# Linear attention with a gated MLP on one core: a padded room in SBUF, gates stored from ScalarE's queue, and a third of wo loaded a round ahead

## The chip, the cores and the metric

The kernel runs on one core of a Trainium2 chip. The metric is the device time of one execution in microseconds (us), from the first instruction to the last, with what the device adds around it. TensorE (PE in the profile; its weight loads PEld) multiplies, VectorE (DVE), ScalarE (ACT) and GpSimd (POOL) work elementwise, and DMAs are issued by SyncE (SP) or, here in one stage before the change, by ScalarE. Each engine runs its own instructions in order. Data lies in SBUF, 128 partitions of rows, and matmuls write to PSUM. A matmul has a stationary operand, the weights, and a streamed one, here nearly always 128 partitions by 512 columns of 4 bytes.

## The reference

x is 2048 x 1024; there are 32 heads of 32; the inner width of the MLP is 3584.

```python
x = A_x
xn = _layernorm(x, axis=-1)
s = _A_ref(xn, A_wqkv, A_w_phi, A_wo)
g = _silu(_B_ref(xn, B_w1, B_w3, B_w2))
return x + s * g
```

`_A_ref` projects to q, k and v, maps q and k by a matrix for each head and a softmax of the result and of its negative (64 features), sums kv = phi_k^T v and z = sum of phi_k over all positions, and returns (phi_q kv) / (phi_q z + 1e-6) times wo. There is no causal mask. `_B_ref` is silu(xn w1) * (xn w3) times w2. Everything is float32.

## The kernel before

**Products.** A float32 number is split into a high part and a rest (`split`), and a product is three matmuls (`PASSES`: high by high, high by low, low by high). On top of that all large products use a two by two scheme with seven block products in place of eight. `ORDER` names them: left factors A11, A12, S2, S1, S3, S4, A22, right factors B11, B21, T2, T1, T3, B22, T4, and three PSUM banks a, b, c that sum them.

**Stages.** In order of time: gate and up (`gate_up`, matmuls in line 598), in two halves of tokens, each with 28 blocks of 128 columns of w1 and w3; the streamed operand is the normalized x, seven tiles `op0...` for the first half and `op1...` for the second, and the weights are `bo`. Then the heads in three rounds of eight pairs of token tiles: `heads` twice (line 794, streamed `op2...`, `op3...`, weights `xo`) for k and v, with the small matmuls of `kv` (line 779) between, and `query_heads` (line 861, `op4...`). Then the product with w2 (`product`, line 1195): seven rounds kb of eight pairs i of token tiles, one step for each; the streamed operand is `bo`, tiles of w2, the weights `af`, `as`. A step has seven block products of six matmuls (`TURN`); the products of A11, A12 and S2 belong to the new pair, the other four to the pair before, so that one more step with `new` None follows the last. Last comes attention (`attend`, line 1320) and the product with wo (`out_half`, line 1335), over 16 token tiles t, with 48 matmuls of 512 columns for each.

**Where tiles lie.** SBUF is filled by two stacks, one from each end. In the built program a row of each tile begins at these bytes of a partition; those of one pool follow each other in steps that are multiples of 512:

| pool | side | first byte | past a multiple of 512 | holds |
|---|---|---|---|---|
| misc | left | 1536 | 0 | `ident`, `consts` |
| small | left | 2560 | 0 | `early_z` first, then small tiles |
| work | left | 4992 | 384 | `w` and `h1` tiles, among them `as` for S2 |
| q | left | 19328 | 384 | quads: `bo` of gate and up, `xo`, `af`, `as`, `oT`, `g` |
| big, later acc | left | 64384 | 384 | `op` tiles in homes 0 to 6, later the 16 slabs |
| rb | left | 129920 | 384 | ring slots 8 to 19 |
| spare, later ra | right | 179712 | 0 | `op` tiles in homes 7 and 8, later ring slots 0 to 7 |
| rw | right | 212480 | 0 | raw weights, `ev`, `eq`; later `late` (ring slots 20, 21) and `room` |

`HOMES` says which operand lies where: all of op0 on the left; of op1 A11 and A12 on the right; of op2 T2 and T1; of op3 T3 and B22; of op4 none.

**The ring.** In the w2 stage `ring` hands out 22 slots of 4 KB a row in turn. A round of w2 takes 14. In the last round (kb = 6) the other eight go, in step i = 0, to `e0` (2), `kvs`, `own`, `ez` (2) and `xrs` (2). The 16 tiles of wo (`load_wo`) follow as the tiles of w2 are used up: six in step i = 7, eight in the step without a new pair, and two behind the loop.

**Gates.** The sums of pair i stand in two of the 16 slabs, by `SLABS[i]`. In the last round `gate(i - 2, j)` puts Silu over such a slab on ScalarE and stores it to `g_d` by SyncE, twice a step; those of pair 7 come behind the first attention. `load_g(t)` fetches gate and x of tile t again. Slabs that are free are used again: `load_e` fetches the query features of tile t into two of them, and `turn_e` transposes these into two others, from which `attend` streams.

```python
return slabs[:, (12, 14, 8, 10)[t % 4] + c] if t else e0[c]
```

**Order.** From line 1236 on the order on every engine is the program's own. In tile t of the attention stage stand, one behind the other: `out_half(t, 0)`, `load_e(t + 4)`, `scale` and `turn_e` of t + 1 on VectorE, for t + 3 >= 4 `z_products` on GpSimd, the rest of t - 1 (`gated`, `store_out`), `load_g(t + 1)`, `gated(t, 0)`, and then `attend(t + 1, ...)` around `out_half(t, 1)`; the low parts of `oT` (line 1326) come behind that on VectorE. SyncE issues the loads and stores in the same order, and one that waits holds up all behind it.

`early_z` is the room for the sums over features of the first four tiles (`EARLY`), which are made during the w2 stage. `edge_l` and `edge_r` are unused rooms at the two ends of SBUF; `PAD` is 32 and not used.

Of the kernel before, what the change touches and what calls it, by code (L numbers as in the profile page):

```python
# [8 lines left out]
F = mybir.dt.float32  # L9
# [8 lines left out]
P = 128  # L18
# [7 lines left out]
PAD = 32  # L26
# [3 lines left out]
def tile_kernel(ctx: ExitStack, tc: tile.TileContext, x, wkT, wqT, wv, wphi, wo, w1, w3, w2, out):  # L30
    nc = tc.nc
    open_pools = {}

    def pool(name, bufs, **kw):

        open_pools[name] = tc.tile_pool(name=name, bufs=bufs, reuse_waits="tile", **kw)
        return open_pools[name].__enter__()

    def close(*names):
        for name in names:  # L40
            open_pools.pop(name).__exit__(None, None, None)
# [23 lines left out]
    ANAMES, BNAMES = [n for _, n, _ in ORDER], [n for _, _, n in ORDER]  # L65

    pairs = [(8 * (i // 4) + i % 4, 8 * (i // 4) + i % 4 + 4) for i in range(NT // 2)]
# [3 lines left out]
    g_d = [dram.tile([P, D], F, name=f"g_d{i}") for i in range(NT)]  # L71
# [65 lines left out]
    small = pool("small", 2)  # L137
# [32 lines left out]
    def quad(name, dt=R):  # L170
        return qp.tile([P, 2, 4, P], dt, name=name, tag="q")
# [4 lines left out]
    def flat(t):  # L176
        return t.rearrange("p k t -> p (k t)")
# [1 line left out]
    ident = misc.tile([P, P], F, name="ident")  # L179
    consts = misc.tile([P, P], F, name="consts")  # L180
    eps_t = consts[:, 0:1]
    early_z = small.tile([P, 256], F, name="early_z", bufs=1)
    bd = bdp.tile([P, G, P], F, name="bd")

    def load_x(t, halves):
# [10 lines left out]
    def rstd(mv, sd=None):  # L196

        sd = small.tile([P, 4, 2], F, name="sd") if sd is None else sd
        var = mv[:, :, 1]
        nc.scalar.activation(sd[:, 0], var, AF.Sqrt, bias=eps_t)  # L200
        yield sd
        nc.vector.reciprocal(sd[:, 1], sd[:, 0])

        nc.vector.tensor_mul(sd[:, 2], sd[:, 1], sd[:, 1])
        nc.vector.scalar_tensor_tensor(sd[:, 3], var, EPS, sd[:, 2], op0=OP.add, op1=OP.mult)
        nc.vector.tensor_scalar(sd[:, 3], sd[:, 3], -0.5, 1.5, op0=OP.mult, op1=OP.add)
        nc.vector.tensor_mul(sd[:, 1], sd[:, 1], sd[:, 3])
        yield sd
# [186 lines left out]
    for tb in range(2):  # L395
        for f in range(NF):
            own = [at_event[tb, f, j] for j in range(7)]
# [279 lines left out]
    _, sd = rstd(mvs[0], sds[0])  # L677
# [245 lines left out]
    def ring(name):  # L923
        nonlocal ring_at
        k = ring_at % 22
        ring_at += 1
        if k < 20:
            return (bpa if k < 8 else bpb).tile([P, 2, 512], R, name=name, tag=f"ra{k}" if k < 8 else f"rb{k}")
        return late_rw[0][:, k % 2]
# [104 lines left out]
    bpb = pool("rb", 1)  # L1034
    slabs = accp.tile([P, 16, D], F, name="acc")

    SLABS = ((0, 1), (14, 15), (8, 9), (10, 11), (2, 3), (4, 5), (6, 7), (12, 13))

    def acc_of(i):
        return [slabs[:, m, c * 512:(c + 1) * 512] for m in SLABS[i] for c in range(2)]  # L1040

    for n in range(4, 7):
        load_b(0, n)

    wos, us, ezs = {}, {}, []
    EARLY = 4

    def load_wo(k):
        t = ring("wos")
        nc.sync.dma_start(t.bitcast(F), wo_d[k // 8][k % 8])  # L1050
        wos[k // 8, k % 8] = t

    def gate(i, j):
        m = SLABS[i][j]
        nc.scalar.activation(slabs[:, m], slabs[:, m], AF.Silu)
        nc.sync.dma_start(g_d[pairs[i][j]], slabs[:, m])

    def slot_f(name):
        return flat(ring(name).bitcast(F))

    def strips():
        for a in range(2):
            for s in range(2):
                yield a, s, slice(64 * a + 32 * s, 64 * a + 32 * s + 32)
# [18 lines left out]
    def load_kvs():  # L1083
        kvs = slot_f("kvs")
        for a, s, sl in strips():
            nc.sync.dma_start(kvs[sl].rearrange("p (j n) -> p j n", j=4), kv_d[:, :, s].rearrange("j f c g d -> f j (c g d)"))
        return kvs.rearrange("p (j c g d) -> p j c g d", j=4, c=2, g=4)
# [16 lines left out]
    def col(m):  # L1104
        return own[:, 64 * m:64 * m + 64]
# [44 lines left out]
    def factors(t):  # L1150
        if t < NT:
            nc.gpsimd.tensor_mul(col(0), col(3 + t % 2), w_all[:, 64 * t:64 * t + 64])

    def e_slab(t, c):
        return slabs[:, (12, 14, 8, 10)[t % 4] + c] if t else e0[c]

    def et_slab(t, c):
        return slabs[:, 2 * (t % 4) + c]

    def load_e(t):  # L1160
        for a, s, sl in strips():
            if t:
                m = (12, 14, 8, 10)[t % 4]
                nc.sync.dma_start(slabs[sl, m:m + 2].rearrange("i c (g n) -> i c g n", g=2), e_part(t, a, s))
            else:
                for c in range(2):
                    nc.sync.dma_start(halves(e0[c][sl]), e_part(0, a, s)[:, c])

    def scale(t, c):
        e = by_head(e_slab(t, c))  # L1170
        by = of_half(early(t) if t < EARLY else col(0), c)
        nc.vector.tensor_mul(e, e, by.unsqueeze(3).to_broadcast([P, 2, 16, DH]))
# [36 lines left out]
            nc.vector.tensor_add(c, pb, c)  # L1209


    steps = [(kb, i) for kb in range(NKB) for i in range(len(pairs))] + [None]
    TURN = (ORDER[3], ORDER[0], ORDER[4], ORDER[1], ORDER[5], ORDER[2], ORDER[6])
    FIRST = ("A11", "A12", "S2")
# [4 lines left out]

    for n in range(2 * EARLY):  # L1220
        at_ = 7 * 18 + 21 * n
# [15 lines left out]
    for r, new in enumerate(steps):  # L1237
        kb, i = new or (NKB, 8)
        end = kb >= NKB - 1
        if not end and i in (2, 3, 4, 5):  # L1240
            load_b(kb + 1, i - 2)
        if r + 2 < len(steps) - 1:
            ahead[r + 2] = load_h(*steps[r + 2])
        if r == 2:
            late_rw.append(rwp.tile([P, 2, 2, 512], R, name="late", tag="rw"))
            room_z = rwp.tile([P, 2, D], F, name="room", tag="rw")
            zb, er = room_z[:, 0], room_z[:, 1]
            w_all = er
        if r == 17:
            load_z()  # L1250
        if end:
            if i == 0:
                e0 = [slot_f("e0") for _ in range(2)]
                load_e(0)
                kvs, own = load_kvs(), slot_f("own")
                ezs += [slot_f("ez") for _ in range(2)]
                xrs = [slot_f("xr") for _ in range(2)]
            elif 3 < i < 7:
                load_e(i - 3)
        parts, bank = first, {}  # L1260
        if r and new:
            gen2 = second_parts(*parts)
        if r + 1 < len(steps) - 1:
            gen1 = first_parts(ahead.pop(r + 1))
        if kb and new:
            seed(i, bank, r)
        for m, (b, an, bn) in enumerate(TURN):
            if an in FIRST:
                if new:
                    product(kb, i, bank, r, parts[2], b, an, bn)  # L1270
            elif old:
                product(*old, banks, r, second, b, an, bn)
                if new is None:
                    for k in range(2 * BNAMES.index(bn), 2 * BNAMES.index(bn) + 2):
                        load_wo(k)
            if m < 3 and r and new:
                then = next(gen2)
            if m in (3, 4) and r + 1 < len(steps) - 1:
                first = next(gen1)
            if end and m in (1, 4) and 1 < i:  # L1280
                gate(i - 2, m // 4)
            if i + 1 == len(pairs) and an in FIRST:
                n = BNAMES.index(bn)
                for k in range(2):
                    if end:
                        load_wo(2 * n + k)
                    elif k:
                        load_b(kb + 1, 4 + n)
            for do in pieces.pop(7 * r + m, ()):
                do()  # L1290
        if new:
            second = then if r else ready[1]
        old, banks = new, bank
    for k in range(14, 16):
        load_wo(k)
    assert not pieces
    close("ps")


    ps = pool("ps4", 3, space=PSUM)  # L1300
    oTs, gs = {}, {}

    def load_g(t):
        if t < NT:
            gs[t] = flat(quad("g", F).rearrange("p u k t -> p u (k t)"))
            nc.sync.dma_start(gs[t], g_d[t])
            nc.sync.dma_start(xrs[t % 2], x[t * P:(t + 1) * P, :])


# [46 lines left out]
    for t in range(NT):  # L1356
        p, last = out_half(t, 0), t + 1 == NT
        if t + 4 < NT:
            load_e(t + 4)
        if not last:  # L1360
            for c in range(2):
                scale(t + 1, c)
        if t + 2 >= EARLY:
            weigh(t + 2)
        if not last:
            for c in range(2):
                turn_e(t + 1, c)
        if t + 3 >= EARLY:
            z_products(t + 3)
# [5 lines left out]
        store_out(t, 0)  # L1375
        if t + 2 >= EARLY:
            add_pairs(t + 2)
# [51 lines left out]
```

## Time and profile before

| what | us |
|---|---|
| median of 3 runs | 2409.21 (2408.97 to 2412.23) |
| the profiled execution | 2408.6 |
| its span, first to last instruction | 2406.8 |
| TensorE busy | 2371.8 |
| VectorE busy | 1763.1 |
| ScalarE busy | 909.5 |
| GpSimd busy | 257.2 |

The granted clock of TensorE is 0.999 of full speed over the span. 582 MB pass the DMA engines, 242 GB/s in the mean.

How to read it: a line of a view names an engine, a line of the kernel, and out<-in by the program's tile names without their numbers (op1A is op1A11, op1A12 and op1A22; bo is any tile of that name). Busy time is the union of the instructions' times. A single matmul is shown with some 390 ns, since its own time covers filling and draining the array, and the next one starts long before it ends; the pace is seen from when the next one starts. The chain of waits follows the work that ended last back from the end of the kernel; each piece has its start, its length and how many instructions are merged in it. "issue" is time in which an engine waited for nothing that the profile shows.

### The profile page before, as it was taken

What the parts mean: (1) busy time and instruction counts of PE and PEld (TensorE: products, weight loads), DVE (VectorE), ACT (ScalarE), POOL (GpSimd) and SP (SyncE); (2) the same over time, 40 slices, a digit from 0 to 9 for tenths busy, and PEclk for the clock granted to TensorE, in tenths of its full rate; (3) what the DMA queues carried; (4) which work ended last, traced back from release to release, by engine and by line L of the source; (5) the groups of instructions that cost most, each with busy time, mean ns of one, the idle gap of its engine ahead of it and who ended that gap; (6) DMA issues with size and microseconds to landing.
All of it is one profiled execution on the core that took longest, in us unless ns stands there. A gap on an engine that the chain in (4) does not pass through costs nothing.

```text
span 2406.8 us, 37213 instructions
## 1 busy us (share of the span) xinstructions
PE 2371.8 (99%) x14348; PEld 1934.4 (80%) x14348; DVE 1763.1 (73%) x2729; ACT 909.5 (38%) x1597; POOL 257.2 (11%) x243
## 2 busy tenths in 40 slices
PE   7999999999999999999999999999999999999999
PEld 6888888888788888888788788887888888886887
DVE  8877787765688888874566666786678888785775
ACT  6445454443344445542221212334433333352000
POOL 1000000000000000000000000331012222112662
PEclk9999999999999999999999999999999999999999
DMA  5446799976988888865977878986544554469773
GB/s 213 148 160 203 245 344 338 329 250 193 278 294 289 293 275 295 269 228 190 377 278 288 289 244 320 366 289 239 171 139 133 186 182 141 167 186 309 224 195 119
DMA packets 292625, 582.19 MB, mean 242 GB/s; under 512 B 25041, under 2 KB 140897, under 8 KB 289761
## 3 DMA queue, kind: packets, MB, share of 16 engines
q1 hardware_dynamic: 287840, 563.04, 69.4%
q10 hardware_dynamic: 4608, 16.78, 1.8%
q8 instruction: 113, 1.85, 0.3%
q14 instruction: 64, 0.52, 0.1%
HBM read 374.73 MB, written 205.00 MB: 241 GB/s over the span
## 4 chain that ended last, share of the span: by engine, by line
PE 91%; DMA 3%; DVE 3%; SPq 1%; ACT 1%; issue 1%; POOL 0%; DVEq 0%; ACTq 0%; POOLq 0%
PE bankb L598 24%; PE bankb L1195 13%; PE bankc L598 12%; PE bankb L794 7%; PE pm L1335 6%; PE bankc L1195 6%; PE banka L598 6%; PE bankc L794 3%; PE banka L1195 3%; PE bankb L861 3%; PE banka L794 2%; PE bankc L861 1%; PE pkv L779 1%; PE po L1320 1%; DMA g_d<-acc 1%; PE pw L247 1%
## 5 line engine op out<-in xcount | busy, mean ns | idle before, releaser
L93 DVE TENSOR_TENSOR bo<-rw,bo 128x512 fp32r<-128x512 f32 x336 | 230.8, 689 | 161.5 <-ACT bo L92 160.9
L1195 PE MATMUL bankb<-bo,as 128*128 128x512 f32 x960 | 238.3, 392 | 1.2 <-ACT acc L1201 1.2
L1195 PEld LDWEIGHTS bankb<-bo,as 128*128 128x128 f32 x960 | 180.1, 188 | 42.2 <-ACT acc L1201 1.6
L92 ACT CAST bo<-rw 128x512 fp32r<-128x512 f32 x336 | 206.4, 617 | 14.0 <-DVE w2o L93 4.4
L1335 PE MATMUL pm<-wos,oT 128*128 128x512 f32 x672 | 168.6, 399 | 4.5 <-DMA wos<-wo_d 2.7
L598 PE MATMUL bankb<-op0S,bo 128*128 128x512 f32 x672 | 164.7, 394 | 1.9 <-ACT op0S L92 1.2
L598 PE MATMUL bankb<-op1S,bo 128*128 128x512 f32 x672 | 161.8, 390 | 0.7 <-ACT u L633 0.7
L598 PE MATMUL bankc<-op0S,bo 128*128 128x512 f32 x672 | 162.4, 391 | 0.0
L598 PE MATMUL bankc<-op1S,bo 128*128 128x512 f32 x672 | 161.6, 389 | 0.5 <-DVE bo L93 0.5
L598 PE MATMUL bankb<-op1A,bo 128*128 128x512 f32 x672 | 159.9, 392 | 2.2 <-DVE bo L93 2.2
L598 PE MATMUL bankb<-op0A,bo 128*128 128x512 f32 x672 | 159.8, 392 | 0.8 <-DVE bo L93 0.5
L1195 PE MATMUL bankc<-bo,as 128*128 128x512 f32 x624 | 160.4, 392 | 0.0
L771 POOL MEMSET ev<- 128x32 f32 x32 | 4.1, 129 | 1438.4 <-DVE bo L93 1100.1
L1335 PEld LDWEIGHTS pm<-wos,oT 128*128 128x128 f32 x672 | 123.1, 188 | 36.9 <-DMA wos<-wo_d 5.7
L598 PEld LDWEIGHTS bankb<-op1A,bo 128*128 128x128 f32 x672 | 125.8, 188 | 31.2 <-DVE bo L93 2.6
L598 PEld LDWEIGHTS bankb<-op0S,bo 128*128 128x128 f32 x672 | 126.3, 190 | 29.1 <-ACT op0S L92 1.6
L598 PEld LDWEIGHTS bankb<-op1S,bo 128*128 128x128 f32 x672 | 126.1, 188 | 28.1 <-ACT u L633 1.1
L598 PEld LDWEIGHTS bankc<-op1S,bo 128*128 128x128 f32 x672 | 126.1, 188 | 27.1 <-DVE bo L93 0.9
L598 PEld LDWEIGHTS bankb<-op0A,bo 128*128 128x128 f32 x672 | 125.2, 188 | 27.0 <-DVE bo L93 0.8
L598 PEld LDWEIGHTS bankc<-op0S,bo 128*128 128x128 f32 x672 | 125.4, 188 | 25.8
L1195 PEld LDWEIGHTS bankc<-bo,as 128*128 128x128 f32 x624 | 117.1, 188 | 26.3
L1209 DVE TENSOR_TENSOR acc<-bankb,acc 128x512 f32<-128x512 f32 x152 | 102.4, 684 | 36.2 <-PE bankb L1195 34.6
(260 smaller groups left out, 4348.9 us busy)
## 6 DMA issues: line engine op xcount, KB each, us to landing
rw<-in_w SPq DMA_DIRECT2D x112, 512.0 KB, 4.5
hr<-h_d SPq DMA_DIRECT2D x56, 512.0 KB, 4.8
h_d<-h SPq DMA_DIRECT2D x111, 256.0 KB, 5.1
xoS<-xo_d0S SPq DMA_DIRECT2D x44, 512.0 KB, 6.2
xoS<-xo_d1S SPq DMA_DIRECT2D x44, 512.0 KB, 6.2
xoA<-xo_d0A SPq DMA_DIRECT2D x33, 512.0 KB, 5.1
xoA<-xo_d1A SPq DMA_DIRECT2D x33, 512.0 KB, 4.9
e_d<-eq ACTq DMA_DIRECT2D x32, 512.0 KB, 5.9
```

The source lines that it names most:

```text
L92: nc.scalar.copy(hi, src)
L93: (by or nc.vector).tensor_sub(lo, src, hi.bitcast(F))
L247: nc.tensor.matmul(pw[:, g, :], wr[:, g], bd[:, 4 * c + g, :], start=True, stop=True)
L598: nc.tensor.matmul(bank[b], bos[tb, f][bn][:, w, k], ao[an][:, u, k], start=first and n == 0, stop=LAST[b] == an and n == 11, skip_group_c ...
L771: nc.gpsimd.memset(v[:, :, DH:], 1.0)
L779: nc.tensor.matmul(pkv[sl, m], e[:, m // 4, (m % 4) * P + 32 * h:(m % 4) * P + 32 * h + 32], v[:, 4 * (m % 4) + h], start=first and m == 0 ...
L794: nc.tensor.matmul(bank[b], xo[an][:, u, k], wb[bn][:, w, k], start=an in ("A11", "A12", "S1") and n == 0, stop=LAST[b] == an and n == 11, ...
L861: nc.tensor.matmul(bank[b], xo[an][:, u, k], wb[bn][:, w, k], start=an in ("A11", "A12", "S1") and n == 0, stop=LAST[b] == an and n == 11, ...
L1195: nc.tensor.matmul(bank[b], t[:, u, pos + k], bos[kb, bn, k][:, w], start=first and n == 0, stop=LAST[b] == an and n == 5, skip_group_chec ...
L1209: nc.vector.tensor_add(c, pb, c)
L1320: nc.tensor.matmul(po[32 * j:32 * j + 32, a, 64 * k:64 * k + 64], kvs[sl, j, c, k], et[sl, :, 4 * k + j], start=True, stop=True, skip_grou ...
L1335: nc.tensor.matmul(p, oTs[t, h][:, a, k], wos[c, 4 * h + k][:, b], start=n == 0, stop=n == 3 * ND - 1)
```

## The change

`early_z` gets 32 more columns, 128 bytes a row, which are not used. Its pool then takes a multiple of 512 bytes (2560 for 2432), and all that follows it on the left stack moves up by 128 bytes: work, q, big, acc and rb.

The slabs of pair i are now 2i and 2i + 1. The gates of pairs 0 to 5 are stored by ScalarE's own queue, right behind the Silu; those of pairs 6 and 7 (tiles 10, 14, 11 and 15) stay in their slabs, and `load_g` fetches only x for them. The features of tile t (from 1 on) go to slabs 2 to 9 in turn, their transposes to slabs 0 and 1 or 10 and 11. In the last round `load_e(1)` to `load_e(3)` come one step later.

In step i = 0 of the last round the eight other slots go to `e0`, `kvs` and the first five tiles of wo. Six more tiles follow in step i = 7, five in the step without a new pair, and there the slots of the remaining used tiles go to `own` and `ez`; `xrs` come behind the loop.

```diff
-    early_z = small.tile([P, 256], F, name="early_z", bufs=1)
+    early_z = small.tile([P, 256 + PAD], F, name="early_z", bufs=1)[:, :256]
...
-    SLABS = ((0, 1), (14, 15), (8, 9), (10, 11), (2, 3), (4, 5), (6, 7), (12, 13))
-
     def acc_of(i):
-        return [slabs[:, m, c * 512:(c + 1) * 512] for m in SLABS[i] for c in range(2)]
+        return [slabs[:, 2 * i + j, c * 512:(c + 1) * 512] for j in range(2) for c in range(2)]
...
-    EARLY = 4
+    EARLY, KEPT, gs = 4, 6, {}
...
     def gate(i, j):
-        m = SLABS[i][j]
+        m, t = 2 * i + j, pairs[i][j]
         nc.scalar.activation(slabs[:, m], slabs[:, m], AF.Silu)
-        nc.sync.dma_start(g_d[pairs[i][j]], slabs[:, m])
+        if i < KEPT:
+            nc.scalar.dma_start(g_d[t], slabs[:, m])
+        else:
+            gs[t] = slabs[:, m]
...
+    def e_at(t):
+        return 2 + 2 * ((t - 1) % 4)
+
     def e_slab(t, c):
-        return slabs[:, (12, 14, 8, 10)[t % 4] + c] if t else e0[c]
+        return slabs[:, e_at(t) + c] if t else e0[c]

     def et_slab(t, c):
-        return slabs[:, 2 * (t % 4) + c]
+        return slabs[:, (0, 10)[t % 2] + c]
...
+    def late_slots(bn):
+        nonlocal own
+        n = BNAMES.index(bn)
+        if n < 5:
+            for k in range(5 + 2 * n, 7 + 2 * n):
+                load_wo(k)
+        elif n == 5:
+            load_wo(15)
+            own = slot_f("own")
+        else:
+            ezs.extend(slot_f("ez") for _ in range(2))
...
                 load_e(0)
-                kvs, own = load_kvs(), slot_f("own")
-                ezs += [slot_f("ez") for _ in range(2)]
-                xrs = [slot_f("xr") for _ in range(2)]
-            elif 3 < i < 7:
-                load_e(i - 3)
+                kvs = load_kvs()
+                for k in range(5):
+                    load_wo(k)
+            elif 4 < i < 8:
+                load_e(i - 4)
...
                 if new is None:
-                    for k in range(2 * BNAMES.index(bn), 2 * BNAMES.index(bn) + 2):
-                        load_wo(k)
+                    late_slots(bn)
...
                     if end:
-                        load_wo(2 * n + k)
+                        load_wo(5 + 2 * n + k)
...
-    for k in range(14, 16):
-        load_wo(k)
     assert not pieces
+    xrs = [slot_f("xr") for _ in range(2)]
...
     def load_g(t):
         if t < NT:
-            gs[t] = flat(quad("g", F).rearrange("p u k t -> p u (k t)"))
-            nc.sync.dma_start(gs[t], g_d[t])
+            if t not in gs:
+                gs[t] = flat(quad("g", F).rearrange("p u k t -> p u (k t)"))
+                nc.sync.dma_start(gs[t], g_d[t])
             nc.sync.dma_start(xrs[t % 2], x[t * P:(t + 1) * P, :])
```

More of the change, by code (lines that the diff above doesn't have):

```diff
@@ L1162, in load_e @@
             if t:
-                m = (12, 14, 8, 10)[t % 4]
+                m = e_at(t)
                 nc.sync.dma_start(slabs[sl, m:m + 2].rearrange("i c (g n) -> i c g n", g=2), e_part(t, a, s))
@@ L1209, in product @@
             nc.vector.tensor_add(c, pb, c)
+    def late_slots(bn):
[9 more added lines that the diff above has]
+            ezs.extend(slot_f("ez") for _ in range(2))
+    own = None
     steps = [(kb, i) for kb in range(NKB) for i in range(len(pairs))] + [None]
@@ L1293, in tile_kernel @@
         old, banks = new, bank
-    for k in range(14, 16):
-        load_wo(k)
     assert not pieces
+    xrs = [slot_f("xr") for _ in range(2)]
     close("ps")
     ps = pool("ps4", 3, space=PSUM)
-    oTs, gs = {}, {}
+    oTs = {}
     def load_g(t):
         if t < NT:
-            gs[t] = flat(quad("g", F).rearrange("p u k t -> p u (k t)"))
-            nc.sync.dma_start(gs[t], g_d[t])
+            if t not in gs:
+                gs[t] = flat(quad("g", F).rearrange("p u k t -> p u (k t)"))
+                nc.sync.dma_start(gs[t], g_d[t])
             nc.sync.dma_start(xrs[t % 2], x[t * P:(t + 1) * P, :])
```

## The prediction

> **What bounds the kernel now.** I read the page's first line of busy times, then the chain of waits that ended last, stage by stage.
>
> ```profile
> PE 2371.8 (99%) x14348; PEld 1934.4 (80%) x14348; DVE 1763.1 (73%) x2729; ACT 909.5 (38%) x1597; POOL 257.2 (11%) x243
> PE 91%; DMA 3%; DVE 3%; SPq 1%; ACT 1%; issue 1%; POOL 0%; DVEq 0%; ACTq 0%; POOLq 0%
> ```
>
> TensorE is busy 99% of the span and is 91% of the chain. So only two things can move the time by much: the pace of one matmul after another, and the few places where TensorE stands still. I looked for both.
>
> The pace first. In the chain a run of matmuls lasts until the next run starts, so its length divided by its count is the pace. Two windows of the gate and up stage (L598), one in each token half:
>
> ```profile
> 560.28 5.44 PE bankb L598 x24
> 565.72 2.72 PE banka L598 x12
> ...
> 781.25 2.80 PE banka L598 x12
> 784.05 2.73 PE bankb L598 x12
> ...
> 794.94 5.51 PE bankb L598 x24
> ```
>
> The same product A12 (bank a, 12 matmuls of 128x512) takes 2.72 us in the first half and 2.80 in the second: 226.7 against 233.3 ns each. Nothing waits in either. What differs is the place of the streamed operand: in the first half it lies in "big" (left stack of SBUF, rows that start 384 bytes past a multiple of 512), in the second half A11 and A12 lie in "spare" (right stack, rows that start at a multiple of 512). The weights lie in "q", left, at 384, in both. The heads stage (L794) shows the same in one token pair:
>
> ```profile
> 1255.01 2.72 PE banka L794 x12
> 1257.73 2.79 PE bankb L794 x12
> 1260.52 2.81 PE bankc L794 x12
> 1263.33 0.70 PE pkv L779 x59
> 1264.02 2.93 PE bankb L794 x12
> 1266.95 2.72 PE bankc L794 x12
> ```
>
> B21 (big, left) 2.72; T2 and T1 (spare, right) 2.79 and 2.81; T3 and B22 (big) again 2.93 and 2.72. The 2.93 follows the many small kv matmuls of L779: a restart costs 0.21 us even when the operand is on the left. The group rows of S1 by T1 in the two rounds of this stage agree, since T1 changes its place between them:
>
> ```profile
> L794 PE MATMUL bankc<-op2T,xoS 128*128 128x512 f32 x96 | 23.7, 395 | 0.0
> ...
> L794 PE MATMUL bankc<-op3T,xoS 128*128 128x512 f32 x96 | 23.1, 389 | 0.0
> ```
>
> It is slow in round 0 (op2, right) and fast in round 1 (op3, left). So it is the place and not the product. Every left operand shares its offset with the weights and runs at 226.7 ns; every right operand stands 128 bytes off and runs near 233.
>
> The standstills next. The longest are where the last product ends and attention starts (windows: span, TensorE busy, ..., granted clock, DMA share, GB/s), with the waits in 2150 to 2250:
>
> ```profile
> 2183.00:2193.00 10.00, 9.51 (x220) 6.93 (x219) 6.62 (x7) 3.66 (x5) 0.00 (x0) 1.00 1.03 418
> 2193.00:2203.00 10.00, 7.75 (x87) 4.47 (x87) 0.00 (x0) 0.58 (x1) 0.00 (x0) 1.00 1.03 417
> ...
> PE pm L1335 <- DMA wos<-wo_d: 2.7, 8, 0.8
> PE pm L1335 <- DVE oT L1326: 1.2, 1, 1.2
> ```
>
> The granted clock is 1.00, so the throttle has no part. The DMA engines are full for 20 us, wo tiles arrive late eight times, and VectorE reaches L1326 late, because the tile g ahead of it came late. The chain shows why:
>
> ```profile
> 2183.19 0.80 PE po L1320 x53
> ...
> 2196.73 10.01 DMA g_d<-acc
> ...
> 2208.71 5.43 DMA acc<-e_d
> ...
> 2224.97 0.85 PE po L1320 x49
> 2225.82 2.99 PE pm L1335 x12
> ...
> 2229.60 8.51 PE pm L1335 x36
> 2238.28 0.79 PE po L1320 x53
> ...
> 2251.52 0.79 PE po L1320 x53
> ```
>
> The last store of a gate takes 10 us in the full DMA queues; load_e(4), which reuses that pair's slabs, waits for them on SyncE, and behind it stand the next g and x.
>
> **The change, part by part.** The profiled execution took 2408.6 us (span 2406.8, 1.8 around it); the median of the runs is 0.6 above. The sum is made on 2408.6.
>
> *The pad.* 128 bytes more in the small pool move everything behind it on the left stack from 384 to 0 past a multiple of 512: work, q, big, acc, rb. The right stack stays at 0. So every streamed operand, left or right, then has the offset of its weights, and I take 226.7 ns for all of them.
> - L598, second half: per block of 128 columns the run with A11 falls from 5.51 to 5.44, A12 from 2.80 to 2.72, the run behind it from 2.73 to 2.72: 0.16 x 28 blocks = 4.5 us.
> - L794: T2 and T1 lose 0.07 + 0.09 = 0.16 in each of 8 pairs, T3 and B22 as much in the second round: 2.6 us.
> - L1195, where tiles of both stacks take turns in the ring. First and last rows of the stage and the starts of bank a in two pairs of neighbouring steps:
>
> ```profile
> L1195 PE MATMUL bankb<-bo,af x288: 387/392/502, 1639.1 to 2170.3; 128*128 128x512 f32 x144
> ...
> 1958.87 1.37 PE banka L1195 x6
> ...
> 1968.53 1.37 PE banka L1195 x6
> ...
> 2142.85 1.40 PE banka L1195 x6
> ...
> 2152.59 1.40 PE banka L1195 x6
> ```
>
> A step of 42 matmuls takes 9.66 or 9.74 us, against 42 x 0.2267 = 9.52; over 56 steps that is 7.8 to 12.3. The whole stage, 1639.1 to 2183.19, is 544.1 us against 2352 x 0.2267 = 533.1; of the 11.0 some waits and the early sums' matmuls stay. I take 9.
> - L1335: a run of 36 takes 8.51 = 3 x 2.72 + 0.21 (restart, as behind kv) + 0.14, a run of 12 takes 2.99 = 2.93 + 0.06; 0.20 x 16 tiles = 3.2. I take 3.
>
> Together 19 us. No trace here shows weights and operand both at 0, so the bounds are wide: with no gain 0, and with the full loss instead (below) minus 47.
>
> A rule of the Trainium skill speaks against this part. Its page "TensorE: Matmul & The Clock Gate", section "Step-by-step: what each phase is for", says that TensorE reads SBUF through two independent ports and that loading the next weights takes no read bandwidth from the matmul that runs. By it the place of an operand could not matter, and the 19 would be 0. The rows of 2.72 and 2.80 do not agree with that.
>
> *Gates by ScalarE's queue.* Twelve stores leave SyncE's queue. ScalarE already issues stores of this size in the query stage:
>
> ```profile
> L846 ACTq DMA_DIRECT2D e_d<-eq x32: 326/326/345, 1494.7 to 1646.3; - x32
> ...
> 2156.35 0.58 ACT L1184 COPY banka<-acc 128x512 f32<-128x512 f32 x1
> ...
> 2162.16 1.56 PE L1195 MATMUL banka<-late,af 128*128 128x512 f32 x6
> ```
>
> Each costs 0.33 us of ScalarE, and a short wait until its own Silu has written: 12 x 0.33 = 4 us of an engine that is 38% busy. Queued behind it are the seed of bank a and casts for the next step; the seed ends at 2156.93 and TensorE wants it at 2162.16. That slack of 5.2 us hides it: 0. Without cover it would be at most the 4 us. SyncE no longer stands in front of a Silu, so its e and h loads go out earlier, if anything.
>
> *Four gates kept, slabs renumbered, five wo tiles a round ahead.*
>
> ```profile
> 2111.00 0.99 SPq L942 DMA_DIRECT2D hr<-h_d  x2
> ...
> 2174.03 1.06 ACT L1055 ACTIVATE acc<-acc 128x1024 f32<-128x1024 f32 x1
> ...
> 2188.37 2.36 DVE L1175 STREAM_TRANSPOSE acc<-acc 128x1024 f32<-128x1024 f32 x2
> ...
> L1050 SPq DMA_DIRECT2D wos<-wo_d x14: 319/320/739, 2172.7 to 2191.8; - x14
> ...
> DMA to landing us min/median/max: 3.0/5.6/10.6
> ```
>
> Four stores and four loads of 512 KB go. load_e(4) now reuses pair 4's slabs, stored two steps earlier. The transposes of e(1) go into pair 5's slabs, whose second Silu ends at 2175.1; they ran at 2188.4 before, so there are 13 us for a store of g_d, which took up to 10.6 (last row). The five wo tiles go out ahead of two h loads that were issued at 2111.0. At up to 0.74 us for an issue h is 3.7 us later; it took no more than the 10.6 of the stores to land, and its first user stands behind bank a of step 50, two steps before the 2142.85 above, so at 2123.4: at 2125.3 in the worst case, 1.9 us late for ScalarE and VectorE, which work for the step after; 0 for TensorE. In the last step eleven tiles remain, and the last of them is issued where tile 11 was before.
>
> What it is worth: from the first to the fourth attend the old chain takes 2224.97 - 2183.19 = 41.8 us. Without waits that is 2 x 0.79 + 24 matmuls (two thirds of 8.51) = 7.3, and two tiles of 13.24 (2251.52 - 2238.28): 33.8. So 8.0 us are lost there, of which the idle rows name 2.7 + 1.2. I take 7 (bounds 2.7 and 8.0): e(4), g(0) and the wo tiles all come earlier than their users, but the DMA queue is still well filled until about 2195. Next late would be e(4) for GpSimd.
>
> Sum: 2408.6 - 19 - 7 = 2382.6, say 2383.
>
> **The rivals.**
> 1. *The offset itself is what is slow, not the difference.* If an operand row that starts at a multiple of 512 bytes runs at 233 whatever its weights' offset, the pad makes all operands slow. It decides from the first matmul of L598. For it: in this trace the two readings can't be parted, as all weights lie at 384. Against it: the run behind a slow one (2.73) and the run behind kv (2.93) are slow on the left too and settle, so two streams get in each other's way, rather than one start being bad. Price: 9840 matmuls of 512 columns x 0.08/12 = 66, less the 19 that are slow already: +47. 2408.6 + 47 - 7 = 2449.
> 2. *The pad does nothing for pace*, as where two ports never disturb each other and something else about the right stack is slow: 2408.6 - 7 = 2402. This is the result by the skill's rule above. Against it are left and right rows of the same product.
> 3. *The tail's wait moves rather than goes*: the DMA engines stay at 1.03 until 2203 with other tiles in them, or VectorE waits for pair 5's store. Then only the pace counts: 2408.6 - 19 = 2390.
>
> **How the numbers follow.** Forecast 0.70 (own range 2377 to 2390), rival 1 0.10, rival 2 0.11, rival 3 0.09. 2408.6 less 22 (every matmul of L1195 and L1335 improved to the full) and less 8 gives 2379, and some restarts may shrink as well: low 2375. The high end takes in rival 2: 2404. Rival 1 stays outside. Faster by over 0.2% (what a measurement of this kernel can tell) are the forecast, rival 3 and nearly all of rival 2: 0.87; within 0.2%, rival 2 with a smaller tail gain: 0.03; slower 0.10.
>
> **What would show it.** In the chain, bank a of L598 in the second half at 2.72 instead of 2.80 and T1 of the heads at 2.72 (2.80 everywhere is rival 1; unchanged, rival 2). A step of L1195 near 9.52. The wait of L1335 for wo gone, and 34 to 35 us from the first attend to the fourth (41 is rival 3). It would be wrong above all if operand and weights at the same offset 0 do not run as they do at 384.

## The result, and the profile after

The changed kernel takes 2379.76 us (median of 4 runs, 2379.66 to 2381.62) against 2409.27 for the kernel before (4 runs, 2408.97 to 2412.23). The ratio is 0.9877, with a 95% interval of 0.9860 to 0.9894. The forecast was 2383 in a range of 2375 to 2404. The profiled execution took 2381.62 us, with a span of 2379.8 and a granted clock of 0.999.

Two lines of the page of the changed kernel, the busy times and the shares of the chain of waits:

```profile
PE 2351.0 (99%) x14348; PEld 1934.9 (81%) x14348; DVE 1760.9 (74%) x2729; ACT 910.1 (38%) x1597; POOL 257.6 (11%) x243
...
PE 93%; DVE 3%; DMA 2%; ACT 1%; SPq 1%; issue 0%; POOL 0%; DVEq 0%; ACTq 0%; POOLq 0%
```

TensorE has the same 14348 matmuls and is busy 20.8 us less (2351.0 for 2371.8). So most of the gain is pace. The span fell by 27.0, so some 6 us more are time in which TensorE no longer stands still.

The chain of waits of the changed kernel, in the gate and up stage (L598), the heads (L794) and the stage of w2, where `product` is now line 1199:

```profile
655.92 5.44 PE bankb L598 x24
...
794.96 2.72 PE banka L598 x12
...
1113.82 5.44 PE bankb L598 x24
...
1242.87 2.93 PE bankb L794 x12
1245.80 2.72 PE banka L794 x12
1248.52 2.72 PE bankb L794 x12
...
1925.02 1.36 PE banka L1199 x6
...
1934.54 1.36 PE banka L1199 x6
```

Bank a of L598 in the second half takes 2.72 us for 2.80 and the run ahead of it 5.44 for 5.51. In the heads all runs but the one behind the kv matmuls take 2.72. A step of w2, from bank a to bank a, takes 9.52 us for 9.66 or 9.74: exactly 42 times 226.7 ns. In the groups of the changed kernel the slow row of the heads has become like the fast one (23.1 us for 23.7):

```profile
L794 PE MATMUL bankc<-op2T,xoS 128*128 128x512 f32 x96 | 23.1, 389 | 0.0
...
L1199 PE MATMUL bankb<-bo,af x288: 388/389/500, 1629.1 to 2152.3; 128*128 128x512 f32 x144
```

Now the tail: the chain of the changed kernel (`attend` is L1336, `out_half` L1351, the low part of oT L1342, the first `gated` L1359), and its windows (span, TensorE busy, weight loads, VectorE, ScalarE, GpSimd, clock, DMA share, GB/s).

```profile
2164.89 1.64 PE po L1336 x106
2166.53 5.83 PE pm L1351 x24
2172.36 0.79 PE po L1336 x53
...
2179.95 0.16 DVE g L1359
...
2180.55 0.69 DVE oT L1342
...
2181.29 5.30 PE pm L1351 x22
...
2199.74 0.79 PE po L1336 x53
2200.53 2.95 PE pm L1351 x12
...
2204.27 8.43 PE pm L1351 x36
```
```profile
2165.00:2175.00 10.00, 10.00 (x224) 7.86 (x210) 6.55 (x7) 3.67 (x5) 0.00 (x0) 1.00 0.99 384
2175.00:2185.00 10.00, 9.07 (x99) 6.90 (x99) 5.05 (x6) 0.59 (x1) 2.12 (x1) 1.00 1.05 279
```

From 2164.89 to 2199.74 are 34.85 us, the stretch that the prediction called "first to fourth attend" (41.8 before, 33.8 without waits). What is left of the loss stands at 2179.95: VectorE waits there for the gate of tile 0, works on it, and only then makes the low part of oT that TensorE waits for. (The load of that gate goes out at 2167.18. Its landing is not recorded; that it ends the wait is inferred, as the matmuls whose product VectorE needs besides were done at 2172.36.) The DMA engines are still as full (0.99 and 1.05, for 1.03 and 1.03 in the 20 us behind the first attend of before), though they move less (384 and 279 GB/s for 418 and 417), and other transfers come first.

The table divides the spans of all profiled runs by stage, from the first matmul of one group to the first of the next. "a to d" is the stretch just described. The runs e1 to e12 are told below.

| run | to op1 | gate, up 2nd half | heads | queries | w2 | a to d | rest |
|---|---|---|---|---|---|---|---|
| before | 600.9 | 542.7 | 340.5 | 155.0 | 544.1 | 41.85 | 181.8 |
| after | 600.5 | 535.0 | 337.2 | 156.5 | 535.7 | 34.85 | 180.2 |
| e1 pad alone | 599.7 | 534.9 | 338.3 | 156.1 | 535.7 | 42.87 | 180.0 |
| e2 all but the pad | 600.4 | 543.3 | 339.8 | 155.9 | 544.1 | 33.70 | 180.8 |
| e3 right side moved | 600.0 | 538.0 | 338.6 | 155.5 | 535.7 | 42.81 | 181.6 |
| e4 256 bytes apart | 599.8 | 538.4 | 337.3 | 156.3 | 535.7 | 34.40 | 180.3 |
| e5 128, other sign | 601.3 | 542.0 | 340.4 | 155.0 | 544.0 | 33.74 | 180.8 |
| e6 64 | 600.9 | 541.6 | 339.1 | 156.3 | 543.8 | 34.48 | 180.7 |
| e7 32 | 599.6 | 543.2 | 340.6 | 155.0 | 546.7 | 34.71 | 181.5 |
| e8 SyncE stores | 599.6 | 535.3 | 337.0 | 156.1 | 535.7 | 33.65 | 180.1 |
| e9 no gate kept | 599.5 | 536.0 | 337.2 | 155.0 | 535.7 | 40.60 | 180.1 |
| e10 wo late | 600.4 | 537.2 | 338.6 | 156.1 | 535.7 | 41.88 | 180.1 |
| e11 pad, slabs | 600.6 | 534.3 | 337.6 | 156.3 | 535.7 | 41.89 | 180.1 |
| e12 pad, slabs, wo early | 599.9 | 534.1 | 337.9 | 156.4 | 535.7 | 34.31 | 179.4 |

### The profile page after: what moved, and what is told of

Read it like the earlier page. It is cut to its first block, busy times and chain, and to the rows that moved or that the text cites. A ratio compares the mean times of both kernels' runs of the same rounds, so it can differ in the third digit from the quotient of the medians.

```text
span 2379.8 us, 37194 instructions
## 1 busy us (share of the span) xinstructions
PE 2351.0 (99%) x14348; PEld 1934.9 (81%) x14348; DVE 1760.9 (74%) x2729; ACT 910.1 (38%) x1597; POOL 257.6 (11%) x243
## 4 chain that ended last, share of the span: by engine, by line
PE 93%; DVE 3%; DMA 2%; ACT 1%; SPq 1%; issue 0%; POOL 0%; DVEq 0%; ACTq 0%; POOLq 0%
PE bankb L598 24%; PE bankb L1199 13%; PE bankc L598 12%; PE pm L1351 8%; PE bankb L794 7%; PE bankc L1199 6%; PE banka L598 6%; PE bankc L794 3%; PE banka L1199 3%; PE bankb L861 3%; PE banka L794 2%; PE bankc L861 1%; PE po L1336 1%; PE pkv L779 1%; PE pw L247 1%; PE banka L861 1%
## 5 line engine op out<-in xcount | busy, mean ns | idle before, releaser
L1199 PEld LDWEIGHTS bankb<-bo,as 128*128 128x128 f32 x960 | 180.2, 188 | 39.0 <-ACT acc L1205 1.6
L598 PE MATMUL bankb<-op0S,bo 128*128 128x512 f32 x672 | 164.6, 394 | 1.9 <-ACT op0S L92 1.2
L598 PE MATMUL bankc<-op0S,bo 128*128 128x512 f32 x672 | 162.2, 391 | 0.0
L1351 PE MATMUL pm<-wos,oT 128*128 128x512 f32 x672 | 161.1, 394 | 0.9 <-DVE oT L1342 0.9
L598 PE MATMUL bankb<-op1S,bo 128*128 128x512 f32 x672 | 161.4, 389 | 0.6 <-ACT u L633 0.6
L598 PE MATMUL bankc<-op1S,bo 128*128 128x512 f32 x672 | 161.2, 389 | 0.0
L598 PE MATMUL bankb<-op0A,bo 128*128 128x512 f32 x672 | 159.7, 391 | 0.8 <-DVE bo L93 0.5
L598 PE MATMUL bankb<-op1A,bo 128*128 128x512 f32 x672 | 157.6, 390 | 0.0
L598 PEld LDWEIGHTS bankb<-op0S,bo 128*128 128x128 f32 x672 | 126.3, 190 | 29.0 <-ACT op0S L92 1.6
L1351 PEld LDWEIGHTS pm<-wos,oT 128*128 128x128 f32 x672 | 124.7, 188 | 29.5 <-DVE oT L1342 1.7
L598 PEld LDWEIGHTS bankb<-op1A,bo 128*128 128x128 f32 x672 | 125.9, 188 | 27.4 <-DVE u L641 1.3
L598 PEld LDWEIGHTS bankb<-op1S,bo 128*128 128x128 f32 x672 | 126.1, 188 | 27.1 <-ACT u L633 1.0
L598 PEld LDWEIGHTS bankc<-op1S,bo 128*128 128x128 f32 x672 | 126.1, 188 | 26.2
L598 PEld LDWEIGHTS bankb<-op0A,bo 128*128 128x128 f32 x672 | 125.2, 188 | 26.9 <-DVE bo L93 0.8
L598 PEld LDWEIGHTS bankc<-op0S,bo 128*128 128x128 f32 x672 | 125.4, 188 | 25.6
```

The source lines that it names most:

```text
L598: nc.tensor.matmul(bank[b], bos[tb, f][bn][:, w, k], ao[an][:, u, k], start=first and n == 0, stop=LAST[b] == an and n == 11, skip_group_c ...
L1199: nc.tensor.matmul(bank[b], t[:, u, pos + k], bos[kb, bn, k][:, w], start=first and n == 0, stop=LAST[b] == an and n == 5, skip_group_chec ...
L1351: nc.tensor.matmul(p, oTs[t, h][:, a, k], wos[c, 4 * h + k][:, b], start=n == 0, stop=n == 3 * ND - 1)
```

## The experiments

Two questions were open. For the pace: is it the difference between the offsets of weights and streamed operand that counts, or the offset itself, or something else that the pad moves? For the tail: the prediction gave three parts one sum of 7 us (the new slabs, the gates by ScalarE's queue with four of them kept, the early wo) and a reason that leaned on the slabs. Which of them is it? Ratios are to the kernel before on the same chip, with 95% intervals.

### The two halves of the change

e1 is the kernel before with the pad alone, e2 the changed kernel without it.

```diff
-    early_z = small.tile([P, 256], F, name="early_z", bufs=1)
+    early_z = small.tile([P, 256 + PAD], F, name="early_z", bufs=1)[:, :256]
```

> The kernel before with the padded room alone. Theory (a streamed operand is slow where its row starts at another offset, past a multiple of 512 bytes, than the row of its weights): the whole gain in pace and nothing of the gain at the start of attention, so about 2409.3 less 20, 2389; bank a of L598 in the second half at 2.72 us for 12, the way from the first attend to the fourth still near 41. Rival (most of the gain comes from the moved loads and stores, the pace is a by-product): 2400 or more.

> The changed kernel without the pad. Theory: the start of attention gains its 7 us and the pace stays as before, 2402; bank a of L598 in the second half at 2.80 for 12. If the two parts do not add up (an earlier finish of the products is eaten by the same late transfers), this run and the pad alone together gain other than the 27 of the profiles: more than 29 or less than 25.

e1 took 2391.39 us, ratio 0.9919 (0.9904 to 0.9934); e2 2399.82, ratio 0.9953 (0.9936 to 0.9969). Against 2410.16 that is 18.8 and 10.3 us, together 29.1, and the whole change gains 29.5. The mark set beforehand (over 29 is not adding up) went by the 27 us between the two profiles; against the 29.5 of the medians the two halves add up, as far as these runs can tell. The table says the same: e1 has the w2 stage of after and the tail of before, e2 the other way round.

### Difference or offset

e3 is the kernel before with the right stack moved down by 128 bytes and no pad: weights and operands then all lie 384 bytes past a multiple of 512.

```diff
-    edge[1].tile([P, 120], F, name="edge_r")
+    edge[1].tile([P, 152], F, name="edge_r")
```

> The kernel before, with no pad, but the unused room at the right end 128 bytes larger, so that all tiles of both stacks start 384 bytes past a multiple of 512. Theory (the difference of offsets counts): as fast as the pad alone, 2389 within 2, with 2.72 for bank a of L598 in the second half. Rival (rows that start at a multiple of 512, or of 256, bytes are what is good, for matmuls or for DMAs): no gain, 2409, or a loss.

The chain of e3, bank a of the second half:

```profile
797.58 2.72 PE banka L598 x12
```

e3 took 2392.55 us, 1.6 more than the 2391 that was its upper mark, but its ratio, 0.9925 (0.991 to 0.9939), agrees with that of the pad (0.9919), and its w2 stage takes 535.7 us as well. Everything at 384 is as fast as everything at 0. So the offset itself does nothing; what counts is that weights and streamed operand have the same one.

The starts of single matmuls speak against one more rival, that VectorE, ScalarE or DMAs get in the way of TensorE's reads. In the 25 runs of A12 from 650 us on in the kernel before, the steps from one start to the next alternate between 237 or 238 ns and 229 or 230 ns, the same in every run; in the changed kernel all are 226 or 227. The three steps during which VectorE, ScalarE and GpSimd stood idle (229, 237 and 230 ns) keep the beat. Traffic of others changes from run to run and would not leave so even a beat.

### How far apart

In e4 to e7 the changed kernel has another pad, so that the left stack lies 256, 128, 64 or 32 bytes from the right one (128 with the sign opposite to before; 64 and 32 with its sign).

```diff
-    early_z = small.tile([P, 256 + PAD], F, name="early_z", bufs=1)[:, :256]
+    early_z = small.tile([P, 256 + 96], F, name="early_z", bufs=1)[:, :256]
```

with 96 in e4, 64 in e5, 16 in e6 and 24 in e7.

> The changed kernel with a pad of 384 bytes in place of 128: the left stack starts 256 bytes past a multiple of 512, the right one at 0. If any difference of offsets is slow alike: 2400, with 2.80 for bank a of L598 in the second half. If the period is 256 bytes and not 512: as the changed kernel, 2380, with 2.72. Something between says that the size of the difference counts.

> The changed kernel with a pad of 256 bytes: the left stack starts 128 bytes past a multiple of 512, the right one at 0, so a right operand stands 128 bytes before its weights where it stood 128 behind in the kernel before. With 256 apart fast, a period of 256 makes the two the same: 2.80 us for bank a of L598 in the second half and some 2400. If the sign matters (the weights read ahead of the operand or behind it): another length, 2.72 if only one order disturbs.

> The changed kernel with a pad of 64 bytes: left stack at 448, right one at 0, 64 bytes apart. If every distance that is not a multiple of 256 is slow alike: 2.80 us for bank a of L598 in the second half, 2400. If a short distance matters less: between 2.72 and 2.80. If only 128 is slow: 2.72 and 2380.

> The changed kernel with a pad of 96 bytes: left stack at 480, right one at 0, 32 bytes apart, the finest step of these rooms. All distances alike: 2.80 us for bank a of L598 in the second half. The cost grows with the distance: nearer to 2.72 than the run with 64 apart.

The chains, at bank a of the second half and, where it is slow, the run behind it: e4,

```profile
797.70 2.72 PE banka L598 x12
```

e5,

```profile
780.83 2.80 PE banka L598 x12
783.63 2.73 PE bankb L598 x12
```

e6,

```profile
780.92 2.75 PE banka L598 x12
783.67 2.77 PE bankb L598 x12
```

and e7:

```profile
779.88 2.80 PE banka L598 x12
782.68 2.76 PE bankb L598 x12
```

e4 took 2383.38 us, ratio 0.9884 (0.9869 to 0.9898): 256 bytes apart is as good as nothing apart, in this row and in the w2 stage. (In the median it is 3.6 us above the changed kernel, with intervals that overlap; 3.4 of that stand in the second half of gate and up, which varies among aligned kernels too, see below.) e5, e6 and e7, with one execution each and so without an interval, took 2398.9, 2398.61 and 2403.05, near the 2399.82 of e2. The run on bank a taken alone, 64 apart seems milder (2.75), but the run behind it then takes 2.77: the two together are 5.53 in e5, 5.52 in e6 and 5.56 in e7, against 5.44. The w2 stages say the same: 544.0, 543.8 and 546.7 against 535.7. So the loss does not shrink as the two come nearer; 32 apart even costs 2.7 us more in that stage than 128, and it had been expected to lie nearer to 2.72 than 64 did. Within what was tried there is no partial credit: 0 and 256 bytes apart are free, 32, 64 and 128 cost 1.5 to 2.2% of such a pair of runs. The beat of the single steps changes with the distance, though: two steps long at 128 bytes, three at 64 (232, 225 and 229 ns), four at 32 (231, 234, 233 and 235 ns).

### The parts of the tail, taken away one at a time

e8 is the changed kernel with all stores by SyncE. e9 stores all gates and keeps none. e10 has wo, `own`, `ez` and `xrs` in the order of before.

```diff
-            nc.scalar.dma_start(g_d[t], slabs[:, m])
+            nc.sync.dma_start(g_d[t], slabs[:, m])
```
```diff
-    EARLY, KEPT, gs = 4, 6, {}
+    EARLY, KEPT, gs = 4, 8, {}
```
```diff
-                kvs = load_kvs()
-                for k in range(5):
-                    load_wo(k)
+                kvs, own = load_kvs(), slot_f("own")
+                ezs.extend(slot_f("ez") for _ in range(2))
+                xrs = [slot_f("xr") for _ in range(2)]
...
-                    late_slots(bn)
+                    for k in range(2 * BNAMES.index(bn), 2 * BNAMES.index(bn) + 2):
+                        load_wo(k)
...
-                        load_wo(5 + 2 * n + k)
+                        load_wo(2 * n + k)
...
+    for k in range(14, 16):
+        load_wo(k)
     assert not pieces
-    xrs = [slot_f("xr") for _ in range(2)]
```

> The changed kernel with the twelve gate stores back in SyncE's queue; slabs, kept gates and wo tiles as changed. Theory (what counts at the start of attention is that e(4) reuses slabs stored long before, and that less is in the DMA queues): nearly the changed time, at most 1 us more, and about 35 us from the first attend to the fourth. Rival (the queue is what counts, as SyncE stands behind each Silu again and issues e, g and wo late): 2 to 5 us more.

> The changed kernel with all sixteen gates stored, by ScalarE's queue, and fetched again; slabs and wo tiles as changed. Four stores of 512 KB more go out between 2150 and 2170 and two more loads of g fall in the first tiles' stretch. Theory (the reuse of slabs is what held up attention; the traffic of the kept gates is a smaller part): 1 us more than the changed kernel, at most 3, about 36 us from the first attend to the fourth. Rival (traffic counts most): 4 to 7 us more, with wo or g late again.

> The changed kernel with the tiles of wo loaded as before, sixteen in the last two steps; slabs, kept gates and ScalarE's stores as changed. Theory: wo is late for the second half of tile 0 again, as in the kernel before, eight waits and 2 to 4 us more than the changed kernel. Rival (the kept gates free enough of the queue): within 1 us of the changed kernel.

e8 took 2379.21 us, ratio 0.9876 (0.9859 to 0.9892): ScalarE's queue gains nothing. e9 took 2386.76, ratio 0.9907 (0.989 to 0.9923), 7.0 us more than the changed kernel, where at most 3 were expected; its rival's number (4 to 7) came true. e10 took 2391.52, ratio 0.9917 (0.9903 to 0.9932), the same as the pad alone (2391.39) and 11.8 us more than the changed kernel, where 2 to 4 were expected; by the table 7.0 of that are in the stretch a to d. With wo late, the kept gates, the new slabs and ScalarE's queue together are worth 1 us there (41.88 for 42.87). One of the four executions of e10 took 2385.54, so what it loses is not the same each time.

Two parts (e9 and e10) that each seem to carry nearly the whole gain of the tail don't add up. The waits of SyncE's queue from 2100 to 2190 help (issuing engine and line, what it waited for, us in total, times, longest). In the changed kernel the longest, among others:

```profile
SPq L1168 <- DMA g_d<-acc: 16.1, 4, 5.9
...
SPq L1048 <- DMA g_d<-acc: 10.3, 3, 7.6
```

and in e9:

```profile
SPq L1168 <- DMA g_d<-acc: 15.6, 4, 6.0
SPq L1048 <- DMA g_d<-acc: 14.9, 4, 7.3
```

L1168 is `load_e` and L1048 `load_wo`. SyncE waits there for the landing of gates that another queue stores, although a tile of wo goes into slots of the ring, which no gate ever used. In the built program each DMA of either queue takes the next of eight completion counters and waits until the DMA eight before it has landed. The trace of the changed kernel bears this out: its 1304 DMAs stand on eight counters, 163 on each, and in the 810 cases where the landing is recorded the next DMA of the same counter never starts before it. So a store of ScalarE's queue that is late holds up a load of SyncE's that has nothing to do with it. In e9 it is in the chain itself:

```profile
2158.81 1.07 ACT acc L1053
...
2159.90 7.21 DMA g_d<-acc
...
2167.17 0.32 SPq L1048
...
2169.89 11.72 DMA g<-g_d
...
2182.31 0.69 DVE oT L1342
```

A store of 7.21 us, landed at 2167.11, holds up the wo tile that is next on its counter and goes out at 2167.17, and the tiles behind that one. Behind them the gate of tile 0 goes out only at 2169.89 and takes 11.72, and oT's low part comes at 2182.31. In e8 no wait of `load_wo` or `load_e` for a gate is among the ten longest of SyncE's queue; instead it waits for the Silus, 41.8 us in 11 waits, and the kernel loses nothing by it:

```profile
SPq L1055 <- ACT acc L1053: 41.8, 11, 8.9
```

This gives a theory in which the kept gates only repair what ScalarE's queue costs, and a rival in which they are needed in any case.

### The parts, put together again

e11 has the pad and the new slabs alone: stores by SyncE, no gate kept, wo late (the edits of e8, e9 and e10 together). e12 is e8 with no gate kept, so pad, slabs and the early wo.

> The kernel with the pad and the slabs numbered anew alone: all sixteen gates stored and fetched again by SyncE, wo loaded as before. Beside the run with the pad alone it shows what the slabs alone are worth. Theory: half or more of the 7 us at the start of attention, as e(4) no longer waits for the last stores: 2383 to 2387, some 38 us from the first attend to the fourth, the waits for wo still there. Rival (each of the three has to be there, as the queue is full without the others): within 2 us of the pad alone.

> The changed kernel with all sixteen gates stored by SyncE and fetched again: neither of the gates' parts, only slabs, wo tiles and the pad. Against the run with none kept but ScalarE's stores (2386.8, 40.6 us from the first attend to the fourth). Theory (there SyncE's wo loads stood behind ScalarE's stores, 14.9 us of waits by the waits view, and g(0) behind them): without ScalarE's queue g(0) goes out some 4 us earlier and most of the loss goes: 2380 to 2383, 34 to 37 us. Rival (the four stores and loads of the kept gates fill the DMA engines, whichever queue they are in): 2385 to 2388, 39 to 41 us.

The chain of e11 and its waits from 2160 to 2202 (`attend` is L1338 there, `out_half` L1353, the low part of oT L1344, `gated` L1361):

```profile
2165.27 11.38 DMA wos<-wo_d
...
2176.67 9.91 DMA g<-g_d
...
2187.28 0.69 DVE oT L1344
...
2188.02 5.27 PE pm L1353 x22
...
2206.66 0.79 PE po L1338 x53
```
```profile
DVE g L1361 <- DMA g<-g_d: 16.7, 2, 14.4
PE pm L1353 <- DMA wos<-wo_d: 4.3, 10, 0.9
```

The chain of e12:

```profile
2159.30 9.26 DMA wos<-wo_d
...
2168.57 9.96 DMA g<-g_d
...
2179.23 0.69 DVE oT L1342
...
2179.96 5.28 PE pm L1351 x22
...
2198.32 0.79 PE po L1336 x53
```

e11 took 2388.5 us, ratio 0.9909 (0.9895 to 0.9924). The theory that the slabs give half of the tail's gain or more falls: from the first attend to the fourth it takes 41.89 us, 1 less than with the pad alone. e12 took 2379.35, ratio 0.9868 (0.9852 to 0.9885), a to d 34.31. The step from e11 to e12 is the early wo alone, and it is worth 7.6 us of the tail. Nor are the kept gates needed where SyncE stores.

The two chains have the same links: a wo tile lands, behind it SyncE issues the gate of tile 0, which takes 10 us in the full queues, and VectorE makes the low part of oT after it. The gate is the eighth DMA behind that tile, so by the eight counters it goes out when the tile has landed (2165.27 + 11.38 in e11, 2159.30 + 9.26 in e12). In e11 it goes out at 2176.67, in e12 at 2168.57, 8.1 us sooner, of which 0.8 are the earlier end of the w2 stage. Five wo tiles of 512 KB are 2.6 MB; at the 418 GB/s that these queues moved in the window 2183 to 2193 of before that is 6.3 us of transfer that no longer stands ahead of the gate.

So pad, slabs and early wo give the whole gain, and e12 does without two of the change's parts. It isn't measurably faster than the changed kernel (0.9868 and 0.9877, with intervals that overlap). The early wo with the old slabs was not tried, so whether the new slabs are needed beside it stays open.

## Why the prediction was right

**Pace, 19 us forecast.** The mechanism holds as it was put: same offset, 226.7 ns; 128 bytes apart, about 233. e1 alone gains 18.8. That this lies so close to 19 is in part luck: the terms that the pad explains come to between 17 and 18 (4.3, some 3, 8.4 and 1.9), and the rest is a handover that varies by itself. The terms one by one:

- *L598, 4.5.* By the chain, from 660.30 to 1121.86 before (the run of 24 ahead of A12) and 655.92 to 1113.82 after, 24 blocks of the second half took 461.56 and 457.90 us. That is 0.153 a block, 4.3 for 28, against 0.16 forecast. The rows of before:

```profile
660.30 5.51 PE bankb L598 x24
...
1121.86 5.51 PE bankb L598 x24
```

  The stage as a whole gained 7.7, so 3.4 more came at its start, where op1 takes over (600 to 640). Before, one wait of 2.2 us stood there, and none after:

```profile
PE bankb L598 <- DVE bo L93: 2.2, 1, 2.2
```

  This is not the pad's doing, as far as the runs tell: e3 and e4 are aligned and took 538.0 and 538.4 for the stage, against 534.1 to 537.2 of the other aligned runs. What sets this handover stays open; it varies from run to run by about as much as it gave here.
- *L794, 2.6.* The heads went from 340.5 to 337.2, 3.3 less, but the stages of other aligned runs lie between 337.0 and 338.6 and the query stage took 1.5 more. The row of T1 (23.7 to 23.1) is as forecast.
- *L1195, 9.* The w2 stage fell from 544.1 to 535.7, so 8.4, and to 535.7 in every aligned run. It now stands 2.6 above 2352 x 0.2267 = 533.1.
- *L1335, 3.* Too large. The run of 36 went from 8.51 to 8.43 and that of 12 from 2.99 to 2.95: 0.12 for each of 16 tiles, 1.9 us; the rest of the span fell by 1.6. The step at fault is "3 x 2.72 + 0.21 (restart) + 0.14": the restart behind the small matmuls of `attend` costs 0.27 here (8.43 - 8.16) and not 0.21 as behind kv, so less was left for the offset.

**The rule of the two ports.** By the section "Step-by-step: what each phase is for" of the page "TensorE: Matmul & The Clock Gate" of the Trainium skill, loading weights takes nothing from the matmul that runs; that was rival 2, with 2402. e3 speaks against the rule here: no instruction, queue or side of SBUF is exchanged, only 128 bytes, and the kernel gains 0.75%. Rival 1 (offset 0 slow in itself) falls by the changed kernel and by e3 from two sides. Why 256 bytes is the period, and in what the two reads collide, no trace shows.

**The tail, 7 us forecast.** It gained 7.0, and rival 3 (the wait only moves) did not come about. But the reason given was partly wrong, so that the sum came out to the tenth is luck. The sentence at fault is "e(4), g(0) and the wo tiles all come earlier than their users", with the chain of before (the store of a gate, then `load_e(4)`) shown as what holds the tail up. The new slabs do take that link out of the chain, and e11 shows what is late next: not e(4) for GpSimd, as the prediction had it, but wo and, behind it, the gate of tile 0, with 41.89 us as before. The forecast of rival 3 was then true of every version with new slabs and late wo (e10, e11). With the new slabs in place, what decides is the early wo, which the prediction had as one of three.

**Gates by ScalarE's queue, 0 forecast.** Right for the time, e8 differs by less than its interval, but the working looked in one place only. It counted ScalarE's slack and said that SyncE's loads would go out "earlier, if anything". They do not: SyncE trades its waits for Silu for waits for ScalarE's stores. Where no gate is kept that costs 6.3 us from the first attend to the fourth (e9 40.60, e12 34.31); with four stores fewer, 1.2 (34.85 and e8's 33.65). The section "Issuing engines are not separate DMA queues" of the page "DMA: Bandwidth & Descriptors" of the Trainium skill says that issuing from several engines saves only the time of the issue. The runs agree that there was no more to gain (2379.76 us with ScalarE's queue, 2379.21 without), and the traces show a cost besides.

**h behind the five wo tiles, 0 for TensorE.** This held: the step of w2 is 9.52 at its place and the stage the same as without the early wo (535.7 in e1 and e11, and in e12, which has it).

## What to carry to other kernels

Where a busy TensorE runs some per cent apart on the same product with operands in different places, compare the byte offsets of weights and streamed operand before anything else; here each of the places tried would do in which the two were equal modulo 256 bytes (both at 0, both at 384, 256 apart), and a pad of 128 bytes gained 0.8%. Before counting a wait as gained, ask what is next in the same queue: one removed at the start of attention gave 1 us until the transfers ahead of it were moved too. And a store that is given to another engine's queue may still hold up the first one's loads, so the waits of both queues are read after such a move.

## What the hardware showed that was not expected

- The pace of float32 matmuls of 128x512 depends on the difference of two offsets with a period of 256 bytes: 226.7 ns at 0 and 256, 230 to 232 at 32, 64 and 128 (5.52 to 5.56 us over two runs of 12), with no gain for being near. The step from one matmul to the next keeps an even beat (238 and 229 ns in turn at 128 bytes), whatever the other engines do.
- The loss is shared between a run and the one behind it in a way that changes with the distance: 2.80 and 2.73 at 128, 2.75 and 2.77 at 64, 2.80 and 2.76 at 32. Reading one run alone would mislead.
- Loads of wo by SyncE waited 10.3 us in total (14.9 in e9) for stores of another queue whose data they do not touch. The built program has eight completion counters for both queues, so in full queues, at some 10 us a transfer, a load goes out when the DMA eight before it lands.
